# Attention over groups of two heads instead of four, with even and odd key tiles summed apart

## The chip, the cores and the metric

The kernel runs on one core of a Trainium2 chip. Its time is the device time of one execution in microseconds; the median of three runs is what is compared. The core's engines work from their own queues, in order: TensorE (PE, with its weight loads shown as PEld), VectorE (DVE), ScalarE (ACT), GpSimd (POOL), and SyncE (SP), which here issues every copy between memories. Engines wait for one another by semaphores. TensorE writes to eight banks of accumulators, PSUM; everything else stands in SBUF.

## What is computed

One transformer-like block on 2048 tokens of width 512: layer norm, attention with 32 heads of width 16 that share one key and one value projection, and beside it a two-layer network with Mish whose output gates the attention.

```python
x = A_x                                    # [1, 2048, 512]
xn = _layernorm(x, axis=-1)
# attention: q has 32 heads of 16, k and v have one
q = (xn @ wq).reshape(B, S, 32, 16).transpose(0, 2, 1, 3)
k, v = xn @ wk, xn @ wv
scores = einsum("bhqd,bkd->bhqk", q, k) * 16 ** -0.5
s = einsum("bhqk,bkd->bhqd", softmax(scores), v) -> [B, S, 512] @ wo
# network: 512 -> 1792 -> 512
h = xn @ w1 + b1
g = silu((h * tanh(softplus(h))) @ w2)
return x + s * g
```

## The kernel before

**Tiling.** Tokens are cut into four chunks of 512 queries (`NC`). In each chunk the 32 heads are cut into eight groups of four, so there are `NU` = 32 groups, numbered `v`. A group works through the 16 tiles of 128 keys, one tile per *step*: 512 steps in all. A step has four score matmuls (`e_one`, line 875: 128 keys by 512 queries, one per head), four exponentials on ScalarE (line 877), which write `pt`, and four matmuls with the values (`pv`, line 949) for the step two before. `vaug` holds, beside the 16 columns of the values, columns of ones, so the same matmul gives the softmax's denominator. The four heads of a group stand in four column tiles of 32 rows in one PSUM bank, called `pv`, and add up over 16 steps.

**Queries of a group.** `qts` are three buffers `[128, 2, 512]`. A head is addressed by a side `a` (rows 0 to 63 or 64 to 127) and a part `p` (the middle index). In its 64 rows stand 16 rows of the high part of q, twice, 16 rows of the low part, and two rows that hold the negative maximum of every query. Since those rows meet ones in `ks`, the score matmul subtracts the maximum by itself.

**Maxima.** They have to be known before the scores, so the kernel computes scores twice: `m_one` (line 895) makes 128 queries by 512 keys, and VectorE reduces them (`mb`, line 899), 64 times per group, 2048 in all. This runs `LEAD` = 22 steps ahead of the scores: two maxima per side and step, four a step. Once a group's maxima are there, `c_rows` reduces them over the four key blocks (line 918), splits them into two parts (921, 923), transposes them (928) and has SP move them into `qts` with eight small copies (line 936). The first maxima, 2 x 22 per side, are made ahead of step 0, in the *lead*. Their order (`MSEQ`) is: eight per side for group 0 and eight for group 1, which need only the first 512 keys, then the rest of group 0, then the rest of group 1.

**Lead.** Before step 0, x is loaded, normalised and transposed, and keys and values are projected for chunk after chunk of 512 tokens. A small planner in the program lists these as tasks with an engine, a length and what they depend on, and lays them out by estimated time; a maximum goes in where it fits, a piece of projection otherwise, and a warm matmul (line 1178) if nothing is left. `E0` = 86.0 is the planner's estimate of when step 0 starts; work that is due at a step is placed by it.

**Projections.** All other matmuls (q, w1, w2, wo; called X, tile `xps`) are spread over the steps as half matmuls of 64 rows (`waves`, line 109), six to eight a step, next to the scores or maxima of the other 64 rows. In steps without maxima (the last `LEAD`) they run as full matmuls, four a step (line 105). A queue holds them in order; a group of them begins only when its weights and inputs are ready by the planner's account. ScalarE takes the results out, POOL does most of the elementwise work behind it (Mish, splitting numbers into two parts, line 153 and 148), in order.

**End of a group.** After the last `pv` matmul, `o_out` copies the bank to `os` on ScalarE (line 958), and SP places it with eight copies (line 967) into `oc` (sums) and `sc` (denominators), two groups filling the 128 rows. Then ScalarE takes the reciprocal as exp(-ln) (973, 977) and POOL multiplies and splits. The last group goes another way: `o_last` sorts its rows with eight small matmuls by a permutation, `turns` (1012).

**Order.** Every queue is filled in program order by the loop over steps. A step emits: what is due by then (`timed`), scores and maxima woven with a chunk of X, up to two ScalarE jobs, `pv`, the end of a group where there is one, one piece of `c_rows` if no X result was just taken by VectorE, then weight loads.

Of the kernel before, what the change touches and what calls it, by code (L numbers as in the profile page):

```python
# [20 lines left out]
P = 128  # L21
# [11 lines left out]
NU = 8 * NC  # L33
LEAD = 22
NWARM = 30
E0 = 86.0
# [19 lines left out]
MSEQ = ([(0, n) for n in range(8)] + [(1, n) for n in range(8)]  # L56
        + [(0, n) for n in range(8, 32)] + [(1, n) for n in range(8, 32)])


def m_need(v):  # L60

    return (40, 64)[v] if v < 2 else 32 * (v + 1)
# [53 lines left out]
def block_kernel(ctx: ExitStack, tc: tile.TileContext, x, wq, wk, wv, wo, w1, b1, w2, out):  # L116
# [55 lines left out]
    two = cp.tile([P, 1], F32, name="two")  # L172
    dve.memset(two, 2.0)
    one = cp.tile([P, 1], F32, name="one")
    dve.memset(one, 1.0)
    wk3 = sb.tile([P, 2, NDT, 64], F32R, tag="oc", name="wk3", bufs=1)
    wkf = sb.tile([P, NDT, 64], F32, tag="os", name="wkf", bufs=1)
    ks = cp.tile([P, S], F32R, name="ks")
    pool.memset(f(ks), 1.0)
    vaug = cp.tile([P, NKT, 32], F32, name="vaug")  # L180
# [23 lines left out]
    def load_x(c):  # L204
        for tt in range(4):
            tag, n = ("pt", NPT) if 4 * c + tt < NPT else (("y0", "sc")[tt % 2], 1)
            xin[c, tt] = sb.tile([P, D], F32, tag=tag, name=f"xin{c}_{tt}", bufs=n)
            sp.dma_start(xin[c, tt], xr[4 * c + tt])
# [369 lines left out]
    qt_of = {}  # L578
    xt_done = {}

    def q_group(c, b):
        it = item("wq", ("q", b), wq[:, P * b:P * (b + 1)].rearrange("(t p) n -> p t n", p=P))

        def post(ps):
# [12 lines left out]
            for k in range(2):  # L597
                v = 8 * c + 2 * b + k

                def dmas(v=v, k=k, parts=((0, 0), (0, 1), (1, 0), (1, 1))):  # L600
                    q = qt_of[v] = qts[v % 3]
                    for p, a in parts:
                        o = 64 * a
                        r = 64 * k + 16 * (2 * p + a)
                        for d, src in ((o, qh), (o + 16, qh), (o + 32, ql)):
                            sp_at(0.63)
                            sp.dma_start(f(q[d:d + 16, p]), f(src[r:r + 16]))
                if first:
                    lead["qdma"](lambda ps, dmas=dmas: dmas(parts=[(p, a) for p in ps for a in range(2)]))
                else:  # L610
                    for n in range(4):
                        at(16 * v - LEAD - 9 + 2 * n, lambda dmas=dmas, n=n: dmas(parts=(divmod(n, 2),)))
# [3 lines left out]
                     [lambda: 32 * (4 * c + b) - LEAD - 18, lambda: xt_done.get(c)])  # L616
# [27 lines left out]
    def m1_group(c, ft):  # L644
        it = item("ws", ("1", ft), w1[:, P * ft:P * (ft + 1)].rearrange("(t p) n -> p t n", p=P))

        def post(ps):
# [28 lines left out]
            def st4():  # L676
                if extra(c, ft) == 0:
                    a = sb.tile([P, 2, C], F32R, tag="wq", name=f"act{c}_{ft}", bufs=1)
                elif extra(c, ft) == 1:
                    a = qts[(NU - 3) % 3]  # L680
# [10 lines left out]
        def slot():  # L691
            if extra(c, ft) >= 0:
                return 16 * (NU - 2) * extra(c, ft)
# [149 lines left out]
    for c in range(NC):  # L843
        for k in range(3):
            a = take(2)
            if k == 1 and 1 <= c < NC - 1:
                xt_loads(c + 1, a)
            if k == 0 and c > 0:
                queue.extend(wo_groups(c - 1))
# [14 lines left out]
    def e_one(s, i):  # L864

        v, r = divmod(s, 16)
        if s < NS - LEAD:
            a, k, p = 1 - s % 2, r - r % 2 + i // 2, i % 2
# [483 lines left out]
```

## Time and profile before

| | |
|---|---|
| median of three runs | 1615.79 us (1614.04 to 1616.74) |
| span of the profiled execution | 1612.9 us |
| TensorE busy | 1594.2 us (99%), weight loads 851.9 us |
| VectorE, ScalarE, GpSimd busy | 1348.5, 1294.7, 620.8 us |
| maxima on VectorE (line 899) | 2048, 1272.8 us busy |
| exponentials on ScalarE (line 877) | 2048, 1068.4 us busy |
| granted TensorE clock | 0.999 |

The profile gives for its execution only the span, from the first to the last instruction, and no time of its own. A row of a group of instructions reads: line, engine, operation, out<-in, shape, count, busy time, mean ns of one, idle time before it and what ended that. A row of the timeline begins with the start in us from the start of the span, and the duration. A row of a window reads: the window, its length, then busy time and count for TensorE and its weight loads (or the engine asked for), the granted clock, the share of DMA and GB/s. An `x8` that stands for eight records of `pv` is four matmuls: the trace shows two records for each.

### The profile page before, as it was taken

How to read it: one execution, taken by the hardware profiler on the slowest of the kernel's cores; microseconds unless marked ns; L12 is line 12 of the kernel's file. 1: busy time of each engine (PE TensorE's matmuls, PEld its weight loads, DVE VectorE, ACT ScalarE, POOL GpSimd, SP SyncE). 2: the span in 40 equal slices, each digit the busy share in tenths (PEclk: the TensorE clock that was granted, in tenths of full speed). 3: DMA queues.
4: the chain of work that ended last, by engine and by line, in shares of the span. 5: the costliest groups of instructions: out<-in, count | busy, mean ns of one | idle time of the engine just before them, and what ended most of it. 6: DMA issues, size and time to landing. Idle time of an engine off the chain costs nothing.

```text
span 1612.9 us, 31471 instructions
## 1 busy us (share of the span) xinstructions
PE 1594.2 (99%) x11615; PEld 851.9 (53%) x11615; DVE 1348.5 (84%) x2300; ACT 1294.7 (80%) x2490; POOL 620.8 (38%) x627
## 2 busy tenths in 40 slices
PE   8999999999999999999999999999999999999998
PEld 5455545555555555555555555555555555555534
DVE  8988888888988888888898988888889898888802
ACT  5478788788888778877988787797788878879885
POOL 3875176166265103421524133154153223315522
PEclk9999999999999999999999999999999999999999
DMA  5332133042231304212113321231241313022020
GB/s 161 145 115 64 41 122 111 15 148 83 70 114 52 109 23 153 70 31 91 52 27 111 92 75 26 91 119 38 67 135 34 113 57 96 23 73 78 21 86 26
DMA packets 72776, 127.30 MB, mean 79 GB/s; under 512 B 21488, under 2 KB 34288, under 8 KB 72112
## 3 DMA queue, kind: packets, MB, share of 16 engines
q1 hardware_dynamic: 72624, 125.30, 24.9%
q8 instruction: 92, 1.51, 0.4%
q14 instruction: 60, 0.49, 0.1%
HBM read 76.36 MB, written 27.26 MB: 64 GB/s over the span
## 4 chain that ended last, share of the span: by engine, by line
PE 95%; DVE 2%; ACT 1%; DMA 1%; issue 0%; POOL 0%; SPq 0%; DVEq 0%; ACTq 0%; POOLq 0%
PE xps L109 46%; PE pv L949 31%; PE m L895 8%; PE e L875 5%; PE xps L105 3%; DVE mb L899 1%; PE wop L105 1%; PE warm L1178 0%; PE kp L289 0%; ACT xin L194 0%; DMA xin<-in_dram 0%; DVE st L214 0%; DMA ws<-w 0%; DVE xin L240 0%; PE xp L250 0%
## 5 line engine op out<-in xcount | busy, mean ns | idle before, releaser
L899 DVE TENSOR_REDUCE mb<-m 128x1 f32<-128x512 f32 x2048 | 1272.8, 683 | 184.4 <-PE m L895 157.5
L877 ACT ACTIVATE pt<-e 128x512 f32<-128x512 f32 x2048 | 1068.4, 604 | 253.0 <-PE e L875 236.8
L895 PE MATMUL m<-ks,qt 48*128 48x512 f32 (+1 forms) x2048 | 837.4, 422 | 3.0 <-DVE mb L899 2.5
L875 PE MATMUL e<-qt,ks 64*128 64x512 f32 x2048 | 746.4, 410 | 0.0
L949 PE MATMUL pv<-pt,vaug 128*32 128x512 f32 x4096 | 545.3, 605 | 0.0
L895 PEld LDWEIGHTS m<-ks,qt 48*128 48x128 f32 (+1 forms) x2048 | 370.6, 185 | 67.2 <-DVE mb L899 35.2
L875 PEld LDWEIGHTS e<-qt,ks 64*128 64x128 f32 x2048 | 370.7, 186 | 26.3 <-ACT pt L877 19.6
L109 PE MATMUL xps<-xt,ws 64*128 64x512 f32 x1248 | 345.8, 410 | 0.4 <-POOL ws L153 0.2
L109 PEld LDWEIGHTS xps<-xt,ws 64*128 64x128 f32 x1248 | 215.2, 185 | 205.9 <-ACT pt L877 135.2
L109 PE MATMUL xps<-wbs,act 64*128 64x512 f32 x1158 | 312.9, 407 | 0.1
L109 PEld LDWEIGHTS xps<-wbs,act 64*128 64x128 f32 x1158 | 201.9, 185 | 166.8 <-ACT pt L877 101.5
L949 PEld LDWEIGHTS pv<-pt,vaug 128*32 128x32 f32 x4096 | 80.7, 108 | 141.9 <-issue 133.2
L163 POOL TENSOR_SCALAR t<-t 128x512 f32<-128x512 f32 x56 | 34.5, 616 | 278.4 <-ACT t L658 278.4
L153 POOL TENSOR_TENSOR hb<-hb,t 128x512 f32<-128x512 f32 x56 | 72.3, 1292 | 152.4 <-PE m L895 74.0
L109 PE MATMUL xps<-xt,wq 64*128 64x512 f32 x336 | 93.0, 409 | 0.0
L109 PEld LDWEIGHTS xps<-xt,wq 64*128 64x128 f32 x336 | 58.0, 185 | 55.4 <-ACT pt L877 35.2
L109 PE MATMUL xps<-wbs,ot_all 64*128 64x512 f32 x288 | 79.3, 407 | 0.0
L109 PEld LDWEIGHTS xps<-wbs,ot_all 64*128 64x128 f32 x288 | 49.5, 184 | 47.2 <-ACT pt L877 30.2
L153 POOL TENSOR_TENSOR hb<-hb,u 128x512 f32<-128x512 f32 x56 | 72.3, 1291 | 4.4
L153 POOL TENSOR_TENSOR u<-u,t 128x512 f32<-128x512 f32 x56 | 71.9, 1284 | 4.7
L153 POOL TENSOR_TENSOR act<-hb,act 128x512 fp32r<-128x512 f32 x55 | 70.9, 1289 | 4.6
L721 DVE TENSOR_TENSOR y<-xps,y 128x512 f32<-128x512 f32 x32 | 21.9, 683 | 58.0 <-PE xps L105 58.0
(116 smaller groups left out, 826.7 us busy)
## 6 DMA issues: line engine op xcount, KB each, us to landing
ws<-w SPq DMA_DIRECT2D x38, 512.0 KB
wbs<-w SPq DMA_DIRECT2D x36, 512.0 KB
qt<-qh SPq DMA_DIRECT2D x256, 32.0 KB
w<-ws SPq DMA_DIRECT2D x14, 512.0 KB
w<-wbs SPq DMA_DIRECT2D x14, 512.0 KB
wq<-wq SPq DMA_DIRECT2D x13, 512.0 KB
wbs<-wo SPq DMA_DIRECT2D x12, 512.0 KB
rawwb<-in_dram SPq DMA_DIRECT2D x20, 256.0 KB
```

The costliest lines, as they stand in the source:

```text
L105: self.pe.matmul(ps, self.lhs(), self.rhs(), start=(self.k == 0), stop=(self.k == self.tot - 1))
L109: i = self.pe.matmul(ps, self.lhs()[o], self.rhs()[o], start=(self.k == 0 and self.halves == 0), stop=(self.k == self.tot - 1 and self.hal ...
L153: eng.tensor_tensor(out=o, in0=a, in1=b, op=op)
L163: pool.tensor_scalar(o, o, lim, 0.0, op0=ALU.min, op1=ALU.max)
L721: dve.tensor_tensor(out=y, in0=ps, in1=y, op=ALU.add)
L875: pe.matmul(e, ks[o:o + 64, P * k:P * (k + 1)], q[o:o + 64, p], start=True, stop=True)
L877: r = act.activation(pt, e, AF.Exp, scale=0.25)
L895: pe.matmul(m, q[o, p, P * t:P * (t + 1)], ks[o, C * kb:C * (kb + 1)], start=True, stop=True)
L899: return dve.reduce_max(out=mb_of[v][:, kb, z:z + 1], in_=m, axis=AX.X)
L949: pe.matmul(o[32 * j:32 * j + 32], vaug[:, k], pt, start=(k == 0), stop=(k == 15))
```

## The change

Groups have two heads instead of four: `NU` is 64, and a group takes `GS` = 8 steps. The two heads stand on the two sides; the four matmuls of a step are now two key tiles by two heads, and the part `p` of a column tile is the parity of the key tile. So even and odd key tiles are summed in different column tiles of `pv`, and `o_out` has to add the two: SP copies the upper 64 rows of `os` to a new tile `od`, POOL adds it, and SP places the sum with four copies. Four groups fill the 128 rows of `oc` and `sc`, which have two buffers each now. `c_rows` runs 64 times, each time for half as many maxima, with eight copies again. Maxima run `LEAD` = 14 steps ahead; the first ones in `MSEQ` are four per side for group 0, four for group 1, then the rest of each. A query projection also waits until the fourth group of the one before has been sent to `qts` (`sent`), whose three tiles now serve six groups. `wo_groups` is queued ahead of two `m1` groups instead of behind them. `E0` is 68.0, `two` and `one` share a tile, and the scratch for dynamic DMA is set to 2048.

```diff
-NU = 8 * NC
-LEAD = 22
+NU = 16 * NC
+GS = 8
+LEAD = 14
-E0 = 86.0
+E0 = 68.0
-MSEQ = ([(0, n) for n in range(8)] + [(1, n) for n in range(8)]
-        + [(0, n) for n in range(8, 32)] + [(1, n) for n in range(8, 32)])
+MSEQ = ([(0, n) for n in range(4)] + [(1, n) for n in range(4)]
+        + [(0, n) for n in range(4, 16)] + [(1, n) for n in range(4, 16)])
...
     def q_group(c, b):
...
-            for k in range(2):
-                v = 8 * c + 2 * b + k
+            for k in range(4):
+                v = 16 * c + 4 * b + k
-                    for p, a in parts:
+                    q = qt_of[v] = qts[v // 2 % 3][:, v % 2]
+                    for a in sides:
...
+                    if 1 in sides:
+                        sent[v] = step[0]
...
-                    for n in range(4):
-                        at(16 * v - LEAD - 9 + 2 * n, lambda dmas=dmas, n=n: dmas(parts=(divmod(n, 2),)))
+                    for n in range(2):
+                        at(GS * v - LEAD - 9 + 2 * n, lambda dmas=dmas, n=n: dmas(sides=(n,)))
...
-                     [lambda: 32 * (4 * c + b) - LEAD - 18, lambda: xt_done.get(c)])
+                     [lambda: 32 * (4 * c + b) - LEAD - 18, lambda: sent.get(16 * c + 4 * b - 1), lambda: xt_done.get(c)])
...
     def e_one(s, i):
-        v, r = divmod(s, 16)
+        v, r = divmod(s, GS)
         if s < NS - LEAD:
-            a, k, p = 1 - s % 2, r - r % 2 + i // 2, i % 2
+            a, k = 1 - s % 2, 2 * (r - r % 2) + i
...
     def c_rows(v):
...
-                    sp.dma_start(f(q[r:r + 2]).rearrange("o p (t b n) -> b o (p t) n", b=4, n=32)[b],
-                                 cr[32 * b + 16 * a:32 * b + 16 * a + 16])
+                    sp.dma_start(f(q[r:r + 2]).rearrange("o (t b n) -> b o t n", b=4, n=32)[b],
+                                 cr[32 * b + 16 * a:32 * b + 16 * a + 8])
...
     def pv(s):
...
-                pt = pt_of.pop((s, p, a))
+                pt = pt_of.pop((v, 2 * k + p, a))
                 j = 2 * p + a
-                pe.matmul(o[32 * j:32 * j + 32], vaug[:, k], pt, start=(k == 0), stop=(k == 15))
+                pe.matmul(o[32 * j:32 * j + 32], vaug[:, 2 * k + p], pt, start=(k == 0), stop=(k == GS - 1))
...
     def o_out(v):
...
-        for e, t in ((16, sc), (0, oc)):
-            for j in range(4):
-                r = 64 * k + 16 * j
-                sp_at(0.63)
-                sp.dma_start(t[r:r + 16], os_[32 * j + e:32 * j + e + 16])
+        sp_at(0.63)
+        sp.dma_start(od, os_[HALF:P])
+
+        def both():
+            ew(pool, os_[0:HALF], os_[0:HALF], od, ALU.add)
+            at(pool_at(0.3), place)
+
+        def place():
+            for e, t in ((16, sc), (0, oc)):
+                for a in range(2):
+                    r = 32 * k + 16 * a
+                    sp_at(0.63)
+                    sp.dma_start(t[r:r + 16], os_[32 * a + e:32 * a + e + 16])
+            if k == 3 or v == NU - 2:
+                later(2, lambda: job(n0))
+        later(1.5, both)
```

117 lines of the change are left out of this document (60 added, 57 removed).

## The prediction

> **What bounds the kernel now.** I read the page first: spans, shares and the chain that ended last.
>
> ```profile
> span 1612.9 us, 31471 instructions
> ...
> PE 1594.2 (99%) x11615; PEld 851.9 (53%) x11615; DVE 1348.5 (84%) x2300; ACT 1294.7 (80%) x2490; POOL 620.8 (38%) x627
> ...
> PE 95%; DVE 2%; ACT 1%; DMA 1%; issue 0%; POOL 0%; SPq 0%; DVEq 0%; ACTq 0%; POOLq 0%
> ```
>
> TensorE is on the chain for 95% of the span. As the page itself warns that a busy PE need not be at its peak, I then read single steps. Each step ends with one cluster of eight `pv` records, so the distance of two clusters is a step. Next come the count of these records up to the first step without maxima, and windows cut from one cluster to the next: five steps with maxima, their projection matmuls (L109) counted, and two of the tail with theirs (L105; the count to take is that of the weight loads, behind the second busy time).
>
> ```profile
> L949 PE MATMUL pv<-pt,vaug x3896: 592/605/617, 96.9 to 1525.0; 128*32 128x512 f32 x195
> ...
> 226.96:229.67 2.71, 0.00 (x0) 0.00 (x0) 1.00 0.11 32
> 1205.98:1208.84 2.86, 1.66 (x6) 1.03 (x6) 1.00 0.03 6
> 1214.61:1217.46 2.85, 1.66 (x6) 1.04 (x6) 1.00 0.30 70
> 1223.20:1226.11 2.91, 1.67 (x6) 1.03 (x6) 1.00 0.02 6
> 212.31:215.64 3.33, 1.93 (x6) 0.95 (x6) 1.00 0.16 21
> ...
> 1527.42:1530.21 2.79, 1.13 (x4) 0.68 (x4) 1.00 0.00 0
> 1535.77:1538.32 2.55, 0.96 (x4) 0.49 (x3) 1.00 0.00 0
> ```
>
> 3896 / 8 = 487 steps with maxima from 96.9 to 1527.4: 2.94 us each. A step without projection work still takes 2.71; one with six half-matmuls takes 2.85. A tail step (no maxima, four full projection matmuls) takes 2.79; with three, 2.55, so one more full matmul there is worth 0.24 us.
>
> Last I read the lead, what runs before step 0, on VectorE:
>
> ```profile
> 29.00:90.10 61.10, 53.90 (x88) 1.00 0.33 114
> ...
> 56.40 4.74 DVE L899 TENSOR_REDUCE mb<-m 128x1 f32<-128x512 f32 x7
> 61.06 0.67 DVE L153 TENSOR_TENSOR ks<-kp,ks 16x512 fp32r<-16x512 f32 x1
> ...
> 65.38 18.01 DVE L899 TENSOR_REDUCE mb<-m 128x1 f32<-128x512 f32 x30
> 83.42 0.26 DVE L918 TENSOR_REDUCE mp<-mb 128x16 f32<-128x64 f32 x1
> ...
> 84.14 0.21 DVE L928 STREAM_TRANSPOSE cr<-mp 128x32 f32<-128x32 f32 x1
> 85.55 4.87 DVE L899 TENSOR_REDUCE mb<-m 128x1 f32<-128x512 f32 x8 [1.20 <-PE m L895]
> ...
> 61.76 0.51 SPq L304 DMA_DIRECT2D ks<-ks  x1
> ...
> 74.58 0.38 SPq L439 DMA_DIRECT2D rawwq<-in_dram  x1
> ...
> 77.61 0.63 ACT L395 ACTIVATE wq<-rawwq 128x512 fp32r<-128x512 f32 x1 [0.29 <-DMA rawwq<-in_dram]
> ...
> 90.29 0.47 PE L875 MATMUL e<-qt,ks 64*128 64x512 f32 x1
> ```
>
> The 88 maxima of the lead take 53.9 of its last 61.1 us (0.60 to 0.61 each), and the first scores start at 90.29, with the last of them. Until then the lead is VectorE's; behind it the time is TensorE's, step by step.
>
> **The change, part by part.** *Shorter lead.* 2 x 2 x 22 = 88 maxima become 2 x 2 x 14 = 56. If VectorE stays as full as now, 32 x 0.605 = 19.4 us go; that is one bound. But the new order has only 8 pairs of maxima on the first key block, then 4 pairs each on blocks two, three and four, all of the first group, and only then 8 pairs of the second. So it will wait for the fourth block, which the old order reached late (its last 16 reduces end at 83.42, so started near 73.7). That block's keys leave VectorE at 61.73, are issued at 61.76 and are usable when they land, near 64.3: an estimate, as no row shows it; a weight of 256 KB issued at 74.58 was waited for until 77.61, 3.0 us, and this copy is smaller. From there: 8 reduces, 4.9 us; the row chain 83.42 to 84.35, 0.9; the 1.2 us restart in the quoted row; 16 reduces, 9.7. That is 81.0 against 85.55 + 4.87 = 90.4, a gain of 9.4: the other bound. The fourth block should come sooner, because its subtraction at 61.06 stood behind seven reduces from 56.40, and the links before it behind others. I take 61 instead of 64.3, so first scores at 77.6: **-12.7**.
>
> What is late next is the fourth key block and behind it TensorE's projection of it. TensorE fills its wait with projections and warm matmuls.
>
> *Eight tail steps become steps with maxima.* 512 steps stay, 498 instead of 490 of them with maxima: 8 x (2.94 - 2.79) = **+1.2**.
>
> *Projection work displaced.* The rows for halves in the steps and for the lead:
>
> ```profile
> L109 PE MATMUL xps<-xt,ws 64*128 64x512 f32 x1248 | 345.8, 410 | 0.4 <-POOL ws L153 0.2 <-DMA ws<-w 0.2
> ...
> L109 PE MATMUL xps<-wbs,act 64*128 64x512 f32 x1158 | 312.9, 407 | 0.1
> ...
> L109 PE MATMUL xps<-xt,wq 64*128 64x512 f32 x336 | 93.0, 409 | 0.0
> ...
> L109 PE MATMUL xps<-wbs,ot_all 64*128 64x512 f32 x288 | 79.3, 407 | 0.0
> ...
> L105 PE MATMUL xps<-xt,wq x24: 392/397/502, 16.5 to 70.2; 128*128 128x512 f32 x24
> ```
>
> 3030 halves in 490 steps are 3.1 full matmuls a step. Eight tail steps held 30 (4, 4, 4, 3 by turns), eight new ones hold 25, so 5 are left over. The lead now runs two query projections (24); the second must wait for the `sent` stamp of the fourth group (step 3), so 12 leave the lead, unless another projection fills their place: I take 6. 11 at 0.24 us: **+2.6** (5 to 17 matmuls: +1.2 to +4.1; in steps that now hold none they would cost half as much).
>
> *Group ends.* 32 more of everything that a group does once:
>
> ```profile
> 1207.30 0.18 DVE L923 TENSOR_REDUCE mp<-mp 128x16 f32<-128x32 f32 x1
> ...
> 1209.95 0.20 DVE L928 STREAM_TRANSPOSE cr<-mp 128x32 f32<-128x32 f32 x1
> ...
> 1224.34 0.60 ACT L958 ACTIVATE os<-pv 128x512 f32<-128x512 f32 x1
> ...
> 1210.18 5.33 SPq L936 DMA_DIRECT2D qt<-cr  x8
> ...
> 1218.79 0.40 PE L875 MATMUL e<-qt,ks 64*128 64x512 f32 x1
> ```
>
> The step that holds a row reduce (from 1205.98) took 2.86, the one that holds the copy of `pv` (from 1223.20) 2.91, against 2.85 for the plain one. The 0.9 us chain on VectorE and the 0.6 us copy on ScalarE are hidden by 16 and 20% idle time; 32 groups at 0 to 0.06 us, taken at the middle: **+1.0**. Without that cover they would cost 32 x 1.5 = 48 us, but both engines would have to be full.
>
> *The sum of even and odd key tiles.* Per group: one more copy `od` on SP, one addition on POOL (a 64-partition one takes as long as a full one, 1.28 us in the tail's row below), then four placing copies instead of eight per double group. 63 x 1.28 = 81 us lie in 992 us of POOL's idle time. SP issues 256 more row moves (5.33 / 8 = 0.67 us), and 5 instead of 4 output copies per two heads, taken at the same 0.67: 171 + 42 us of issue, spread over 1500. Query copies stay 12 per four heads. In front of POOL's addition stands the wait for `od`, and behind it the activation chains; in front of SP's placing copies stands that addition, and behind them the row moves of a later group and weight loads. The row moves have room: the transpose ends at 1210.15, first scores come at 1218.79, 8.6 us; only the first four moves (2.7 us) and a landing are needed for them. From the late step below I take **+1.5**, with 0 and the slower rival as ends.
>
> ```profile
> 1559.63 1.28 POOL L153 TENSOR_TENSOR oc<-oc,sc 64x512 f32<-64x512 f32 x1 [17.91 <-ACT sc L977]
> ...
> 212.93 1.29 POOL L153 TENSOR_TENSOR ws<-rawws,ws 128x512 fp32r<-128x512 f32 x1
> ```
>
> The last row is a weight that POOL delivered late: the step from 212.31 took 3.33, 0.48 more than 2.85; three or so more of these, as POOL gets 13% more to do, are the 1.5.
>
> *At nothing:* column tiles for even and odd keys (still four `pv` matmuls and eight records a step), the scores' order, the constants in one tile, the smaller scratch. The final two heads instead of four pass through the same eight small matmuls.
>
> **Sum:** -12.7 + 1.2 + 2.6 + 1.0 + 1.5 = -6.4, so a span of 1606.5. The span shown is 2.9 us below the median of the runs, 1615.79; I take what lies around it as unchanged: **1609.4**.
>
> **Rivals.** *The lead gains all of it.* If the fourth key block comes so early that VectorE never idles, -19.4 instead of -12.7: 1602.7. Against it: each link to that block also passes TensorE and ScalarE, which the change leaves as they are.
>
> *Displaced work is free.* Steps with no projections exist (226.96), and if all 11 land there, at (2.85 - 2.71) / 3 = 0.05 us each, 2.6 becomes 0.5: 1607.3. [...]
>
> *No change.* The fourth block comes no earlier (-9.4), the displaced work costs 4.1, group ends 1.9, late deliveries 2: -0.2, 1615.6.
>
> *Slower: row moves stuck behind the placing copies.* Where SP reaches the placing copies first, it waits there for POOL. If POOL is more than some 3 us late, the rows miss the first scores of the next group, now 64 times. For it, POOL has stretches almost without a break, 28.3 of 32 us in the first row here. Against it, this group's moves came 4.9 us late and the scores still ran at the next step:
>
> ```profile
> 213.00:245.00 32.00, 28.26 (x30) 1.00 0.42 136
> ...
> 219.61 0.20 DVE L928 STREAM_TRANSPOSE cr<-mp 128x32 f32<-128x32 f32 x1
> ...
> 224.72 5.31 SPq L936 DMA_DIRECT2D qt<-cr  x8
> ...
> 230.66 0.49 PE L875 MATMUL e<-qt,ks 64*128 64x512 f32 x1
> ```
>
> It decides from 6.4 / 64 = 0.10 us lost per group; at 0.3 us a group, 19 us, the time is 1609.4 - 1.5 + 19.2 = 1627.1. The Trainium skill, DMA: Bandwidth & Descriptors, section Rules for kernel authors, advises to join small transfers and calls those under 64 KB mostly overhead; the change makes each row move half as large and doubles their number. The quoted eight cost SP 0.67 us apiece, which is in the sum; a landing delay shows in no row.
>
> **How the numbers follow.** The forecast 0.48 (its own range 1604.5 to 1612.5), the full lead 0.12, free displaced work 0.07, no change 0.12 (1612.6 to 1619), slower 0.21 (above 1619). Three runs spread by 2.7 us, so 0.2%, 3.2 us, is about what can be told from no change. Faster holds the first three, 0.67; same 0.12; slower 0.21. The range from 1602 to 1623 leaves out part of the full lead and the upper half of the slower case, about 2 in 10.
>
> **What would show it.** First scores near 77.6 (72 to 81), with an idle stretch on VectorE before the fourth block's reduces. Steps with six halves still at 2.85 to 2.91 on both sides of a group's end. POOL near 700 us, SP's row moves starting within a few us of the transpose. Wrong if first scores stay above 82, if steps at group ends pass 3.0, or if projections remain after the last step.

## The result and the profile after

The changed kernel takes 1623.67 us (median; 1623.09 to 1629.62), against 1616.69 us for the kernel before, run beside it. The ratio estimated from all these runs is 1.0052, with a 95% interval of 1.0035 to 1.0069 (the quotient of the two medians would be 1.0043). The change is slower by half a per cent, where the prediction said 1609.4 us.

The page of the changed kernel, the lines that answer those shown of before:

```profile
span 1621.4 us, 32300 instructions
...
PE 1598.2 (99%) x11647; PEld 858.3 (53%) x11647; DVE 1362.0 (84%) x2428; ACT 1313.8 (81%) x2519; POOL 696.2 (43%) x689
...
PE 95%; DVE 3%; DMA 1%; ACT 1%; issue 0%; SPq 0%; DVEq 0%
```

TensorE is still the chain. POOL came to the 696 us that the sum of the prediction allows, and nothing on this page tells where 8.5 us of span came from. Two marks cut the execution in three: the start of the first and of the last `pv` matmul. First before, then after (records, durations, first and last start):

```profile
L949 PE MATMUL pv<-pt,vaug x4096: 592/593/617, 96.9 to 1592.3; 128*32 128x512 f32 x196
```

```profile
L956 PE MATMUL pv<-pt,vaug x4096: 592/605/1061, 89.8 to 1589.6; 128*32 128x512 f32 x196
```

The lead is 7.1 us shorter. From the first to the last `pv` it takes 1499.8 instead of 1495.4, 4.4 more. Behind the last `pv` stand 1621.4 - 1589.6 = 31.8 us instead of 20.6, **11.2 more**. Sum: +8.5, the difference of the spans. So the end decides.

**The end.** Projections that start behind the last `pv` (before there were none), and the three results that VectorE takes from them:

```profile
L106 PE MATMUL xps<-xt,act x27: 390/398/502, 1590.1 to 1601.9; 128*128 128x512 f32 x27
L106 PE MATMUL xps<-xt,qt x9: 388/393/397, 1594.3 to 1602.6; 128*128 128x512 f32 x9
```

```profile
1595.36 0.69 DVE L729 TENSOR_TENSOR y<-xps,y 128x512 f32<-128x512 f32 x1
1599.20 0.69 DVE L729 TENSOR_TENSOR y<-xps,y 128x512 f32<-128x512 f32 x1 [3.15 <-PE xps L106]
1603.04 0.69 DVE L729 TENSOR_TENSOR y<-xps,y 128x512 f32<-128x512 f32 x1 [3.15 <-PE xps L106]
```

Three whole groups of the second network matrix (3 x 12 = 36 full matmuls) run after attention is done, 3.84 us from one to the next: 0.32 us a matmul, 11.5 us in all. They are made from the last hidden results, and those are late, too. ScalarE began to take the last of the 56 `hb` out of PSUM at 1527.3 before and at 1549.9 after (last start in these rows); counted in `pv` clusters, that is step 497 instead of 487:

```profile
L652 ACT ACTIVATE hb<-xps,b1c x7: 692/692/693, 1442.8 to 1527.3; 128x512 f32<-128x512 f32 x7
```

```profile
L660 ACT ACTIVATE hb<-xps,b1c x7: 687/692/702, 1461.8 to 1549.9; 128x512 f32<-128x512 f32 x7
```

**The lead.** Before the first scores, 48 full matmuls of the first network matrix and 24 of the queries ran; now 36 and 12. Two whole groups, 24 matmuls, left the lead:

```profile
L105 PE MATMUL xps<-xt,ws x48: 390/397/504, 25.2 to 81.5; 128*128 128x512 f32 x48
```

```profile
L106 PE MATMUL xps<-xt,ws x36: 388/398/795, 24.9 to 66.1; 128*128 128x512 f32 x36
L106 PE MATMUL xps<-xt,wq x12: 392/397/497, 16.2 to 18.9; 128*128 128x512 f32 x12
```

Where all the projections went, in full matmuls (two halves count as one), counted in the two traces by the form of the matmul:

| | lead | halves in steps with maxima | full, up to the last `pv` | full, behind it |
|---|---|---|---|---|
| before | 72 | 1515 | 93 | 0 |
| after | 48 | 1539 | 57 | 36 |

The eight steps that became steps with maxima took 24 more, as many as had left the lead. The eight tail steps that were lost had held 36, and as many now run behind the last `pv`.

The changed kernel's timeline of the lead, on SP, TensorE and VectorE (the bracket is idle time before the row and what ended it):

```profile
57.57 0.32 SPq L820 DMA_DIRECT2D xtk<-wbs  x1
57.95 0.44 SPq L444 DMA_DIRECT2D rawws<-in_dram  x1
58.49 0.95 SPq L309 DMA_DIRECT2D ks<-ks  x1
```

```profile
64.12 1.04 PE L902 MATMUL m<-ks,qt 64*128 64x512 f32 x5 [1.70 <-DMA ks<-ks]
...
67.40 5.69 PE L1196 MATMUL warm<-qt 128*128 128x512 f32 x15
...
81.92 0.38 PE L883 MATMUL e<-qt,ks 64*128 64x512 f32 x1
```

```profile
64.66 4.28 DVE L906 TENSOR_REDUCE mb<-m 128x1 f32<-128x512 f32 x7 [1.51 <-PE m L902]
...
73.55 14.64 DVE L906 TENSOR_REDUCE mb<-m 128x1 f32<-128x512 f32 x24 [3.72 <-PE m L902]
```

The copy of the fourth block's keys was issued at 58.49, behind a store of x (1 MB) and the load of a raw weight (256 KB), and waited for until 64.12, 5.6 us. Then the restart behind the row chain took 3.72 us instead of 1.20, since the 15 warm matmuls ran at half clock. Windows of the lead (the granted clock stands behind POOL's busy time):

```profile
64.00:68.00 4.00, 3.88 (x12) 2.10 (x12) 3.34 (x6) 1.22 (x2) 1.47 (x2) 0.61 0.05 10
68.00:72.00 4.00, 4.00 (x11) 2.92 (x10) 1.69 (x6) 2.58 (x5) 3.01 (x3) 0.54 0.00 1
84.00:88.00 4.00, 3.94 (x14) 2.09 (x14) 4.00 (x8) 3.73 (x8) 3.31 (x4) 0.67 0.42 121
88.00:92.00 4.00, 3.95 (x16) 1.10 (x16) 3.03 (x8) 2.30 (x4) 2.95 (x4) 0.50 0.47 124
```

Before, the clock is 1.00 in all of these windows.

**The steps.** Two steps at a group's end, the first with the copy of `pv` on ScalarE (1173.89), the second with the row reduce and POOL's sum (1177.05):

```profile
1172.71:1175.61 2.90, 2.90 (x23) 1.58 (x23) 2.46 (x5) 2.66 (x7) 0.00 (x0) 1.00 0.35 136
1175.61:1178.51 2.90, 2.90 (x24) 1.60 (x23) 2.60 (x6) 2.64 (x7) 1.28 (x1) 1.00 0.94 291
```

2.90, inside the 2.85 to 2.91 that was forecast. One step alone stands out, from 365.7: 5.36 us. SP, POOL and TensorE there:

```profile
361.79 0.33 SPq L446 DMA_DIRECT2D rawwb<-in_dram  x1
...
365.49 5.29 SPq L943 DMA_DIRECT2D qt<-cr  x8
```

```profile
360.49 1.28 POOL L154 TENSOR_TENSOR ws<-rawws,ws 128x512 fp32r<-128x512 f32 x1
```

```profile
369.42 0.46 PE L883 MATMUL e<-qt,ks 64*128 64x512 f32 x1 [2.01 <-DMA qt<-cr]
```

SP had issued nothing since 354.8. It began again with the load of a raw weight, when POOL was done with an earlier one (360.49 + 1.28 = 361.77); then came a store, the four placing copies, and only then the row moves. The first scores of the group waited for those (2.01 us in the last row).

### The profile page after: what moved, and what is told of

Its sections match the earlier page's. It is cut to its first block, busy times and chain, and to the rows that moved or that the text cites. A ratio compares the mean times of both kernels' runs of the same rounds, so it can differ in the third digit from the quotient of the medians.

```text
span 1621.4 us, 32300 instructions
## 1 busy us (share of the span) xinstructions
PE 1598.2 (99%) x11647; PEld 858.3 (53%) x11647; DVE 1362.0 (84%) x2428; ACT 1313.8 (81%) x2519; POOL 696.2 (43%) x689
## 4 chain that ended last, share of the span: by engine, by line
PE 95%; DVE 3%; DMA 1%; ACT 1%; issue 0%; SPq 0%; DVEq 0%
PE xps L110 45%; PE pv L956 32%; PE m L902 9%; PE e L883 6%; PE xps L106 2%; DVE mb L906 1%; PE warm L1196 1%; PE wop L106 1%; PE kp L294 0%; ACT xin L199 0%; DMA ks<-ks 0%; DVE st L219 0%; DMA xin<-in_dram 0%; DVE xin L245 0%; DVE ks L154 0%
## 5 line engine op out<-in xcount | busy, mean ns | idle before, releaser
L902 PE MATMUL m<-ks,qt 48*128 48x512 f32 (+1 forms) x2048 | 848.9, 424 | 4.8 <-DVE mb L906 2.7
L883 PEld LDWEIGHTS e<-qt,ks 64*128 64x128 f32 x2048 | 375.0, 186 | 24.9 <-ACT pt L885 11.7
L110 PE MATMUL xps<-xt,ws 64*128 64x512 f32 x1272 | 353.0, 410 | 0.1
L110 PEld LDWEIGHTS xps<-xt,ws 64*128 64x128 f32 x1272 | 219.1, 185 | 208.8 <-ACT pt L885 138.3
L154 POOL TENSOR_TENSOR os<-os,od 64x512 f32<-64x512 f32 x63 | 81.4, 1292 | 296.5 <-DMA od<-os 171.8
L956 PEld LDWEIGHTS pv<-pt,vaug 128*32 128x32 f32 x4096 | 80.7, 108 | 140.8 <-issue 123.3
L110 PE MATMUL xps<-xt,wq 64*128 64x512 f32 x360 | 100.1, 410 | 0.0
L110 PEld LDWEIGHTS xps<-xt,wq 64*128 64x128 f32 x360 | 62.2, 185 | 60.2 <-ACT pt L885 37.7
```

The costliest lines, as they stand in the source:

```text
L110: i = self.pe.matmul(ps, self.lhs()[o], self.rhs()[o], start=(self.k == 0 and self.halves == 0), stop=(self.k == self.tot - 1 and self.hal ...
L154: eng.tensor_tensor(out=o, in0=a, in1=b, op=op)
L883: pe.matmul(e, ks[o:o + 64, P * k:P * (k + 1)], q[o:o + 64], start=True, stop=True)
L902: pe.matmul(m, q[o, P * t:P * (t + 1)], ks[o, C * kb:C * (kb + 1)], start=True, stop=True)
L956: pe.matmul(o[32 * j:32 * j + 32], vaug[:, 2 * k + p], pt, start=(k == 0), stop=(k == GS - 1))
```

## The experiments

Each run was timed beside runs of the kernel before, which its ratio is taken against. All of them, with the marks of one profiled run of each (us):

| run | median | ratio to before, 95% | first scores | first to last `pv` | behind it |
|---|---|---|---|---|---|
| before | 1616.7 | | 90.3 | 1495.4 | 20.6 |
| the change | 1623.7 | 1.0052 [1.0035, 1.0069] | 81.9 | 1499.8 | 31.8 |
| less_x | 1625.5 | 1.0067 [1.0050, 1.0084] | 79.4 | 1503.9 | 31.8 |
| less_w2 | 1614.1 | 0.9988 [0.9978, 0.9998] | 83.1 | 1502.3 | 20.2 |
| q_lead | 1621.3 | 1.0041 [1.0026, 1.0056] | 80.6 | 1498.5 | 31.8 |
| k_first | 1612.1 | 0.9983 [0.9974, 0.9993] | 78.5 | 1496.4 | 28.0 |
| warm2 | 1625.5 | 1.0062 [1.0047, 1.0077] | 81.6 | 1500.2 | 31.9 |
| banks | 1621.5 | 1.0043 [1.0030, 1.0056] | 80.5 | 1499.9 | 28.5 |
| k_banks | 1612.0 | 0.9975 [0.9966, 0.9984] | 78.3 | 1496.5 | 25.7 |
| store_late | 1624.2 | 1.0054 [1.0037, 1.0070] | 80.4 | 1502.3 | 31.9 |
| sum_dve | 1658.4 | 1.0265 [1.0248, 1.0282] | 83.9 | 1534.6 | 31.8 |
| raw3 | 1620.5 | 1.0033 [1.0022, 1.0045] | 80.7 | 1497.0 | 31.9 |
| lead22 | 1644.9 | 1.0181 [1.0163, 1.0199] | 99.8 | 1505.2 | 28.5 |
| lead22b | 1631.7 | 1.0101 [1.0083, 1.0120] | 95.6 | 1508.5 | 20.1 |
| lead22b_raw3 | 1626.5 | 1.0071 [1.0054, 1.0089] | 94.5 | 1501.7 | 20.2 |
| all4 | 1666.2 | 1.0317 [1.0286, 1.0348] | 77.6 | 1549.6 | 22.9 |

The kernel before took 1614.1 to 1616.7 us (medians) in the sets of runs that these ratios come from. The intervals of less_x, q_lead, warm2, banks, store_late, raw3 and lead22b_raw3 overlap that of the change, so what is said of these rests on their traces, not on their times. The first scores scatter, too: less_x, less_w2, banks, store_late and raw3 run the same instructions in the same order as the change up to there on TensorE and VectorE, and reach them between 79.4 and 83.1.

### Is the end a matter of amount? less_x and less_w2

```diff
 # less_x, in m1_group
+        if c == 1 and 3 <= ft < 6:
+            mms = mms[::3]
...
 # less_w2, in m2_groups
+            if (c, third) == (3, 0):
+                mms = mms[::3]
...
```

> The changed kernel with 24 full projection matmuls left out: in three of the m1 groups of the second chunk only the leading of three partial products is made (4 of 12 matmuls each), so the output lacks the two correction terms there. They lie far ahead of the end. The question is what sets the 11.2 us that the end became longer (32.3 us behind the last pv, against 21.05). Theory 'amount': the end is work that lost its place, each full matmul there costs 0.32 us (3.84 us for a group of 12), so 24 fewer give -7.7 us: about 1616, and 24 to 25 us behind the last pv. Rival 'readiness': the end is set by when the last tile of activations can be made, at step 480, not by how much is queued: 0, still 1623.7, and the 32 us stay.

> The changed kernel with 40 full projection matmuls left out late: the four w2 groups of the last chunk's first third make only the leading of three partial products (5 of 15 matmuls each), so those rows of the output lack the correction terms. In the program's order each takes 2 steps instead of 4, 8 steps in all, and behind them the last m1 groups begin 8 steps earlier, at the step where they begin in the kernel before. Theory 'places': the shorter lead took two projection groups, or 8 steps' worth of places, and the left-out 24 matmuls of the run before made no difference because waits further on took the freed steps up. Then 12 full matmuls stay behind the last pv instead of 36: 24 x 0.32 = 7.7 us less, 1616, some 24 us behind the last pv; and the last m1 result is taken out some 23 us earlier than 1549.9. Rival 'readiness': the end stays at 32 us and 1623.7, whatever is queued ahead.

less_x took away as many matmuls as had left the lead, and the end stayed to a hundredth: 36 matmuls behind the last `pv`, 31.84 us. So the first theory, that each matmul less saves 0.32 us, fell. But the rival, that nothing queued ahead matters, fell with less_w2: 11.7 us less at the end, no projection behind the last `pv` (12 were forecast), and a median of 1614.1, 9.6 us below the change. It leaves out 40 matmuls, not 24; whether 24 at that late place would have been enough was not run. The last `hb` of each, less_x first:

```profile
L660 ACT ACTIVATE hb<-xps,b1c x7: 687/691/701, 1463.4 to 1551.5; 128x512 f32<-128x512 f32 x7
```

```profile
L660 ACT ACTIVATE hb<-xps,b1c x7: 687/692/693, 1439.9 to 1527.2; 128x512 f32<-128x512 f32 x7
```

Both read together: the queue of projections is a timetable. A group takes its place for whole steps (four for 12 or 15 matmuls), and begins only when its buffers and weights are ready. What was saved far ahead was lost at later waits: from one `pv` cluster to the next, the distances without any projection were 13 before, 13 after and 19 in less_x, counted in the traces; at the six to eight halves of a step the six more have room for 18 to 24 matmuls. What was saved late, in less_w2, came out at the end. The two groups out of the lead are eight steps, and the last `hb` was ten steps late; in less_w2 it is at step 488 again. The middle of less_x is 4.1 us longer than that of the change: 2.8 us of it are the stall at 365 us, which takes 5.3 us there (two steps over 2.9) instead of 2.5.

### The second query projection back in the lead: q_lead

```diff
-            qh = sb.tile([P, C], F32R, tag="qh", name=f"qh{c}_{b}", bufs=1)
+            qh = sb.tile([P, C], F32R, tag="qh", name=f"qh{c}_{b}", bufs=2)
 # ql the same
-  [lambda: 32 * (4 * c + b) - LEAD - 18, lambda: sent.get(16 * c + 4 * b - 1), ...]
+  [lambda: 32 * (4 * c + b) - 40, lambda: sent.get(max(16 * c + 4 * b - 5, -1)), ...]
```

> The changed kernel with the start condition of the query projections as it stood before (step 32 x (4c + b) - 40, and the stamp asked for is that of the group whose tiles are overwritten), and two buffers for the split queries, so that the second query projection (12 full matmuls) can run in the lead again, where TensorE waits. Theory 'amount': 12 full matmuls fewer behind the last pv, 12 x 0.32 = 3.8 us: about 1619.9; the first scores stay at 81.9. Rival 'readiness': nothing, 1623.7. If the projection gets in VectorE's way in the lead, first scores come later by up to 12 x 0.24 = 2.9 us and the gain is gone.

60 instead of 48 projections ran in the lead, first scores came no later, and the end did not move: 36 matmuls, 31.8 us. The distances without a projection went to 17. Its median is 2.3 us lower; in its profile 1.3 us of that lie before the first `pv`, inside the scatter of the first scores, and 1.3 in the middle, where the stall at 365 us does not appear. Here one group of the two did not shift the timetable's end.

### Why the fourth key block is late: k_first

```diff
-                kept_0 = task("SP", 0.5, lambda c=c: xt_keep(c, 0), his)
...
+            if c >= 2:
+                kept_0 = task("SP", 0.5, lambda c=c: xt_keep(c, 0), keep_his + [moved] * (c == 3))
+                task("SP", 0.5, keep_low, keep_los + [kept_0])
```

> The changed kernel with the stores of the last chunk's x tiles on SP placed behind the copy that brings the fourth block's keys into place. In the changed kernel that copy is issued at 58.49 us and waited for until 64.12, with two 1 MB stores ahead of it. Theory 'queue': without them it lands some 3 us after it is issued, the fourth block's maxima start about 3 us earlier, first scores at 79 instead of 81.9: about 1621. Rival: the copy takes as long whatever stands ahead of it, and only the stores come later: first scores at 81.9, 1623.7 or more. The planner also puts more projection matmuls into the lead here (some 15 by its own account), so the end may come sooner by up to 15 x 0.32 = 4.8 us; first scores and the time behind the last pv are read apart.

The keys' copy on SP, with a load of a raw weight well ahead of it and the stores behind it; then TensorE and VectorE, and a window of the clock:

```profile
53.38 1.56 SPq L444 DMA_DIRECT2D rawws<-in_dram  x1
...
58.69 0.51 SPq L309 DMA_DIRECT2D ks<-ks  x1
59.25 1.08 SPq L820 DMA_DIRECT2D xtk<-wbs  x2
```

```profile
62.12 0.97 PE L902 MATMUL m<-ks,qt 64*128 64x512 f32 x6
```

```profile
62.67 4.88 DVE L906 TENSOR_REDUCE mb<-m 128x1 f32<-128x512 f32 x8 [3.00 <-PE m L902]
...
70.08 14.44 DVE L906 TENSOR_REDUCE mb<-m 128x1 f32<-128x512 f32 x24 [1.64 <-PE m L902]
```

```profile
68.00:72.00 4.00, 3.57 (x17) 1.92 (x16) 2.30 (x6) 0.63 (x1) 3.66 (x6) 1.00 0.01 2
```

Issued 0.2 us later, the copy was there at most 3.4 us after its issue instead of 5.6, and TensorE no longer waited for it. The Trainium skill, DMA: Bandwidth & Descriptors, section Queues, rings and completion order, says that on each DMA engine the descriptors of a queue are consumed in ring order. The two copies agree with it: by the DMA records of the change, the 8 KB packets of the store start until 62.0, the 512-byte packets of the weight from 61.6 to 63.0 and 2 KB packets, which the keys have, from 62.4; in k_first the keys' packets start at 59.9, with nothing large ahead of them. Store and weight both left the place ahead of the copy, and no run tells their shares apart.

First scores came at 78.5, 11.8 us earlier than before, close to the 77.6 of the prediction, and 3.4 earlier than in the change. Only 1.4 of the 3.4 had been won when the row chain ended (68.4 instead of 69.8). The other 2.1 us are the restart, 1.64 instead of 3.72, at a clock of 1.00; less_x has that clock without this edit, so the edit cannot be said to have brought it. In the profiles k_first is 11.2 us shorter than the change: 4.0 before the first `pv`, 3.4 in the middle, which has no stall at 365 us, and 3.8 at the end, where one group less stands behind the last `pv` (24 matmuls, 28.0 us). Three more projection matmuls ran in the lead (51), and the last `hb` came at step 492 instead of 497. It is the first version that does all the work and is faster than the kernel before, by 0.17%.

### The half clock: warm2

```diff
-        pe.matmul(w, qts[2][:, 0, 0:P], qts[2][:, 0], start=True, stop=True)
+        for _ in range(2 if rows and rows[-1].end is not None else 1):
+            pe.matmul(w, qts[2][:, 0, 0:P], qts[2][:, 0], start=True, stop=True)
```

> The changed kernel with two warm matmuls instead of one wherever the planner puts a warm matmul after the row chain of the first group. Theory 'clock': the granted clock of .50 between 84 and 92 us in the changed kernel follows from too little work of TensorE in the stretch of the last 24 reduces; with more matmuls there the clock stays at 1.0 and the first steps take 2.8 instead of 4.2 us: about -2.6 us, 1621. Rival: the low clock follows from what stands before (the half-clock run of 67 to 73 us) and the added matmuls change nothing or delay the maxima: 1623.7 to 1626.

The clock stayed up (window of warm2), and yet nothing was gained:

```profile
88.00:92.00 4.00, 3.66 (x26) 1.81 (x26) 3.97 (x9) 2.69 (x6) 3.10 (x4) 1.00 0.36 99
```

The twelfth set of four scores came 32.3 us behind the first instead of 33.6; but the added matmuls stood in front of the maxima three times, 1.3 us together, and the stall at 364 us was 3.7 instead of 2.5. So the half clock in 84 to 92 us is worth about 1.4 us by this pair, and this way of avoiding it costs as much.

### The price at the end: banks and k_banks

```diff
+            def alloc():
+                pool_, tag = (ps_m, "m") if step[0] > NS - LEAD else (ps_x, "x")
+                return pool_.tile([P, D], F32, tag=tag, name="xps")
...
```

> The changed kernel with the w2 groups of the last 13 steps and behind them put by turns into the three PSUM banks that the maxima used, instead of one bank for all projections. The amount of work and its order stay. Theory 'price': a full matmul costs 0.32 us behind the last pv because each group waits until VectorE has taken the one before out of the single bank, 0.84 to 0.93 us for a group; with three banks the three groups there cost 12 x 0.24 = 2.9 us each instead of 3.84: -2.9 us, and up to four groups inside the last steps gain up to 0.8 each: 1618 to 1621. Rival: the matmuls themselves take 0.32 us there, whatever the bank: 1623.7.

> Both edits that attack a cause in one kernel: the fourth block's keys copied into place ahead of the x stores (first scores at 78.5, 24 instead of 36 full matmuls behind the last pv, 1612.1 when run alone), and the three banks for the last w2 groups. If the two are independent, 1612.1 less 0.9 us for each of two groups behind the last pv and up to 0.8 for each of four inside the last steps: 1607 to 1610, below both kernels. If the banks gain nothing: 1612.

The results that VectorE takes in the run banks, behind the last `pv`:

```profile
1594.03 0.69 DVE L729 TENSOR_TENSOR y<-xps,y 128x512 f32<-128x512 f32 x1
1596.68 0.69 DVE L729 TENSOR_TENSOR y<-xps,y 128x512 f32<-128x512 f32 x1 [1.96 <-PE xps L106]
1599.48 0.69 DVE L729 TENSOR_TENSOR y<-xps,y 128x512 f32<-128x512 f32 x1 [2.10 <-PE xps L106]
```

2.65 and 2.80 us from one to the next instead of 3.84: with one bank, each group had waited for the evacuation of the one before. 3.3 us came off the end, none off the steps; the median, 1621.5, lies just above the 1618 to 1621 that were forecast. Together with k_first the end is 25.7 us, 2.3 less than in k_first, and the ratio is the lowest here, 0.9975. But the medians of k_first and k_banks, 1612.1 and 1612.0, are the same, where 1607 to 1610 was forecast: the gain of 2.3 us is seen in the two profiles and not in the times.

### The one stall: store_late, sum_dve, raw3

```diff
 # store_late
-        keep_t[0] = max(it.ready + 0.5, keep_t[0] + 2.0)
+        keep_t[0] = max(it.ready + 4.0, keep_t[0] + 2.0)
 # sum_dve
-            ew(pool, os_[0:HALF], os_[0:HALF], od, ALU.add)
-            at(pool_at(0.3), place)
+            ew(dve, os_[0:HALF], os_[0:HALF], od, ALU.add)
+            later(1, place)
 # raw3
-            r = sb.tile([P, D], F32, tag="raw", name=f"raw{tag}{n}", bufs=RAWS)
+            r = sb.tile([P, D], F32, tag="raw", name=f"raw{tag}{n}", bufs=RAWS + 1)
```

> The changed kernel with the stores of split weights (w<-wbs, w<-ws) issued at the earliest 4 steps after POOL's account says that the weight is ready, instead of half a step. The order of the projections stays. In the changed kernel one such store at 362.17 us waited for POOL's split with the placing copies and then the row moves queued behind it on SP, and the step at 365.7 us took 5.36 instead of 2.9. Theory 'SP behind POOL': with the store later, the row moves of that group start when their rows are transposed, the step takes 2.9, and the time falls by 2.4 us or somewhat more: 1620 to 1621.3, with first e to last pv about 1497.5 behind pv 0. Rival: it is the placing copies, which wait for POOL's sum of even and odd keys, that hold the row moves; the stall of 2 us or more stays, 1623.7.

> The changed kernel with the sum of even and odd key tiles on VectorE instead of POOL: 63 additions of 64x512 leave POOL (81 us of its 696), and the placing copies on SP wait for VectorE, one step after the addition. In the program's order the last m1 groups stay where they are (12 steps without a projection, 36 full matmuls behind the last pv). Theory 'POOL's sum': the stall of 2.5 us at 364 to 370 us, which stayed when the weight stores were moved, comes from SP's placing copies waiting for that sum; without it the step takes 2.9 and the time falls by 2.5 us to 1621, less what the additions cost on VectorE (63 x 0.4 to 0.7 = 25 to 44 us in 19% idle time). Rival: POOL is late at that place for what the first chunk gives it (weights to split, m1 results to wait for), SP waits for it with other copies, and the stall stays or VectorE's additions hold up maxima: 1623 to 1627.

> The changed kernel with a third buffer for raw weights; order and counts stay. In the traces so far the first copy on SP that waits ahead of the stalled row moves is each time a load of a raw weight (rawwb), which starts within 0.02 to 0.03 us of the end of POOL's split of the weight before (361.77 and 361.79 us in the changed kernel, 360.82 and 360.85 with late stores, 376.78 and 376.81 with the sum on VectorE). Theory 'raw buffer': with a third buffer that load does not wait, the placing copies and the row moves behind it start some 5 us earlier, the step at 365.7 takes 2.9 instead of 5.36 us: about 1621. Rival: the next copy in SP's queue (a store of a split weight, or the placing copies) waits for POOL as long, and the stall moves or stays: 1623.7.

Neither the store nor the sum was it: the stall stayed, 2.6 us (and 0.8 in the step behind) and 2.9 us. With a third buffer for raw weights SP no longer stopped:

```profile
353.25 0.53 SPq L446 DMA_DIRECT2D rawwb<-in_dram  x1
...
357.12 5.29 SPq L943 DMA_DIRECT2D qt<-cr  x8
```

The row moves start 8.4 us earlier (1.2 of it from an earlier first `pv`), no step of raw3 behind 130 us takes longer than 3.3 us (5.36 in the change), the middle falls from 1499.8 to 1497.0, the median to 1620.5. So it was the load of a weight that waited for POOL to free one of two buffers, with the placing copies and the row moves behind it.

sum_dve missed its forecast by more than 30 us: it is 35 us slower than the change. VectorE waits in its queue for the copy `od`, and TensorE for the maxima behind it (waits of VectorE and of TensorE in sum_dve, then of TensorE in the change: total, times, longest):

```profile
DVE os L154 <- DMA od<-os: 13.8, 6, 6.5
```

```profile
PE m L902 <- DVE mb L906: 24.3, 34, 6.7
```

```profile
PE m L902 <- DVE mb L906: 2.7, 12, 0.3
```

Compared step by step with the change, 31.5 us of the loss lie in the steps that hold the addition, one in eight: 7.2 in one step, in which VectorE waits 6.5 us for `od` (2.2 more in the step behind), and 24 in the others, up to 1.6 us each. Most of those additions wait for nothing. There it is the additions themselves that stand ahead of the maxima, 0.80 us each on average and 50 us in all, or what else shifted; no run tells these apart.

### Grouping alone: lead22, lead22b, lead22b_raw3

```diff
 # lead22b, which also has a third buffer for mb (lead22 keeps 8 pairs on the first block, then group after group)
-LEAD = 14
+LEAD = 22
-E0 = 68.0
+E0 = 86.0
-MSEQ = ([(0, n) for n in range(4)] + [(1, n) for n in range(4)]
-        + [(0, n) for n in range(4, 16)] + [(1, n) for n in range(4, 16)])
+MSEQ = ([(v, n) for v in range(3) for n in range(4)]
+        + [(v, n) for v in range(3) for n in range(4, 16)])
...
```

> Groups of two heads with the old lead of 22 steps (88 maxima, planned start of step 0 at 86, the third group's maxima in the list of first maxima): the grouping alone. Theory 'lead': all of the loss comes from the shorter lead; grouping costs what the prediction said, 1 to 2.5 us: first scores at 90, about 1617 to 1618, some 21 us behind the last pv. Rival 'waits': the grouping itself gives the projections more waits (POOL's added sum per group holds up what they need, and the outputs of a chunk are queued ahead of two m1 groups): by the program's order 22 steps at which no projection can begin, against 12 in both other kernels, and two w2 groups (24 matmuls) behind the last pv: 28 us there, 1623 to 1625.

> Groups of two heads with the old lead of 22 steps again, now with first maxima in an order like the old one: 12 pairs on the first key block (the first three groups), then the rest of the three groups in turn; in lead22 only 8 pairs could run before the fourth block's keys had to be there, and first scores came at 99.8. Theory 'grouping is nearly free': the lead as in the kernel before (first scores 89 to 92), by the program's order 15 steps at which no projection can begin against 12 before and the last m1 groups one step later than before, so hardly anything behind the last pv: 21 to 24 us; steps add 1 to 2.5 us and a row stall or two: 1617 to 1621. Rival 'grouping costs': the steps or stalls of a group of two heads take 5 us or more over all (0.15 us a group more), 1622 and above, of which the changed kernel then hid a part by its shorter lead.

> Groups of two heads with the old lead (lead22b) and a third buffer for raw weights. In lead22b the time from the first to the last pv was 13.0 us longer than before, 9.5 of it in four steps between 360 and 415 us, one of them behind a weight that POOL had not split yet. Theory 'raw buffer': those steps lose their stall, 1622 to 1624, and what the grouping costs over all falls to 3 to 4 us in the steps and 5 us in the lead. Rival: POOL itself is late there, whatever the loads do: 1630 or more.

lead22 came out 20 us above both its forecasts, in part because of its order of maxima: with 88 of them and only 8 pairs that can run early, first scores came at 99.8. 24 matmuls stay behind its last `pv` (28.5 us), and 23 distances hold no projection. lead22b, with the same lead and the other order, has the old end (20.1 us, no projection behind the last `pv`) and 16 such distances. So groups of two heads need not have the longer end: with a long lead and maxima that do not hold it up, the timetable gets its places back. But lead22b is 1.0% slower than the kernel before, on the rival's side. 13.0 us of that lie in the middle, 9.5 of them in four steps between 360 and 415 us; the longest wait of a projection there:

```profile
PE xps L110 <- POOL ws L149: 3.3, 1, 3.3
```

With the third raw buffer 6.8 us of the middle went, and 1501.7 is left against 1495.4; its time, 1626.5, lies above the 1622 to 1624 of the theory and below the 1630 of the rival. About 3.3 of these 6.3 are two steps near 400 us, 1.2 is the last step, which holds a whole group of 12; some 2 us are spread thin. The first scores of lead22b_raw3 came 4.2 us later than before; 12 pairs on the first block, not 16, are there to run while the fourth block's keys are awaited, which was not tried apart.

### Everything at once: all4

k_banks, with the sum on VectorE and four buffers for `hb` (`NHB = 4`).

> Four edits together: the fourth block's keys copied ahead of the x stores, the three banks for the last w2 groups, the sum of even and odd key tiles on VectorE, and four instead of three buffers for the m1 results. In the program's order the last m1 groups begin one step earlier than with the first two edits alone, and 24 full matmuls stay behind the last pv. If the added two are worth what they free, 1610 to 1612, at most 1.5 us below the two edits alone (1612.0); if VectorE is held up by the additions (it is the engine that the maxima wait for), 1613 to 1616.

60 projections in the lead and 12 behind the last `pv`, 22.9 us: the timetable did move. But the time missed the forecast by 50 us, and the middle is 53 us longer than that of k_banks. 45 of these lie in the steps that hold the addition and 8 in those behind them. sum_dve, with that one edit, has 35; why it is 18 more here stays open.

## Why the prediction was wrong

The sum said -6.4, and the profile shows +8.5. Of the 14.9 us between them 8.6 are the end, 5.6 the lead and 0.7 the middle.

**Shorter lead, -12.7.** Measured -8.4 at the first scores and -7.1 at the first `pv`, so this term was too large; kernels with the same order of instructions gave -7.2 to -10.9 at the first scores. The place was right: the fourth key block, with VectorE idle ahead of it. Of "I take 61 instead of 64.3" the 64.3 was right (64.12), though its reason was not: the copy was issued 3.3 us earlier, as the prediction hoped, and then took 5.6 us behind a store and a load. k_first, with the copy ahead of them and at full clock, reaches -11.8. The 1.2 us restart was 3.72 at half clock, which no row of before shows.

**Projection work displaced, +2.6.** This is the step that failed: +11.2, with 36 matmuls behind the last `pv` instead of 11 spread over steps. Three things were wrong in it. The amount: "I take 6" for what leaves the lead was 24, a query group that was not filled in for and an `m1` group; the eight tail steps had held 36, not 30. The form: no lone matmuls moved into steps with room; work moved by groups with places and conditions, so less_x could take 24 matmuls out for nothing and less_w2, with 40 left out late, gain 9.6 us. The price: 0.24 us holds inside a tail step and nearly with three banks (2.65 to 2.80 us for 12), but it is 0.32 behind the last `pv` with one bank. At the price of 0.24 the 36 would have cost 8.6 us, so the amount weighs more than the price. The rival "displaced work is free" erred on the other side.

**Eight tail steps +1.2 and group ends +1.0.** Together no more than about 1 us: k_first, without a stall and at full clock, takes 1496.4 from first to last `pv`, 1.0 more than before. The steps at a group's end were 2.90, as forecast.

**Late deliveries, +1.5.** One stall of 2.5 us, of the slower rival's kind: row moves on SP behind a wait for POOL. The mechanism is real, but its place was wrong (the load of a raw weight, not the placing copies; raw3) and it struck once, not 64 times. With the old lead, taking it away was worth 6.8 us of the middle (lead22b against lead22b_raw3). The slower case came true, and not by the rival that stood for it.

**What it foresaw.** It named "projections remain after the last step" among the signs that would make it wrong, and that sign is the loss. The remaining 1.9 us or so of the middle are not taken apart run by run: the half clock of the first steps (1.4, by warm2) fits, but part of it lies before the first `pv`.

## What to carry to other kernels

Work that fills waits has a place in an order, not only a length: before a lead is shortened, count which whole groups lose their place, follow them to the end, and price them there, by the buffer that each must wait for. Leave work out at two places before calling a queue bound by amount or by readiness; less_x and less_w2 alone would each have told the wrong story. And an engine with 16% idle time is not free: 63 additions of 0.80 us in VectorE's queue, ahead of maxima that TensorE waits for, cost 35 us.

## What the hardware showed

**Half clock on a busy TensorE.** In the changed kernel the clock fell to .61 and .54 between 64 and 72 us, with TensorE busy for 3.88 and 4.00 of 4 us by its records. less_x has the same order of instructions there, and kept it (window, then VectorE's restart):

```profile
68.00:72.00 4.00, 3.69 (x18) 2.48 (x17) 2.28 (x7) 1.49 (x3) 3.83 (x4) 1.00 0.01 3
```

```profile
71.05 2.48 DVE L910 TENSOR_REDUCE mb<-m 128x1 f32<-128x512 f32 x4 [1.58 <-PE m L906]
```

1.58 against 3.72: 2.1 us of the lead hang on it. Six kernels share this order and end the first row chain within 0.6 us of one another. Their first scores come at 79.4 in less_x, 80.4 to 80.7 in store_late, banks and raw3, 81.9 in the change and 83.1 in less_w2; all but less_x show a lowered clock between 64 and 72 us (.64 and .93 in less_w2). The Trainium skill, TensorE: Matmul & The Clock Gate, Part 1: The HAM clock gate, says that the clock halves after an idle window of about 3.4 us, and that the window runs freely, so that where it falls differs from run to run. The spread agrees, and so does the value at the bottom, .50. But the wait of TensorE ahead of the fall is only 1.70 us in the change, and 1.68 in less_x. What TensorE did in the window before, 2.42 us busy of 4 from 60 to 64 and 2.32 in less_x, does not tell the two apart either, and no run here shows what does.

**A small copy behind large ones.** The same copy on the same queue was waited for until 5.6 us after its issue behind a store of 1 MB and a load of 256 KB, and was there within 3.4 us with the stores behind it.
